# Gated mix of a long convolution and local attention: attention steps in another order, feature rows loaded instead of copied, and filters turned by VectorE

## The chip, the cores and the metric

One core of one Trainium2 chip. The metric is device time in microseconds, the median of several executions. A run is called slow when it is over 1.5% above the fastest of its kernel; slow runs stay out of all ratios, but medians and ranges are of all runs.

PE is TensorE, DVE VectorE, ACT ScalarE, POOL GpSimd, SP the engine whose queue issues most DMAs. The granted clock is the share of the full TensorE clock that was granted.

## The reference, cut to what matters

```python
def _A_ref(q, k, v, shift_k, ssm_k, ssm_D):          # S = 2048, D = 640
    k_shift = sum over t of k_pad[:, t:t+S, :] * shift_k[:, 3-t]     # 4-tap convolution
    kv = k_shift * v
    y = irfft(rfft(kv, 2*S) * rfft(ssm_k, 2*S))[:S].astype(bfloat16) # long convolution
    return q * (y + kv * ssm_D)

def _B_ref(x, wqkv, wo):                              # 32 heads of 20
    q, k, v = (x @ wqkv) split by head
    # each position attends to itself and the 7 positions 2, 4, ... 14 before it
    return softmax_attention(q, k, v) @ wo

g = sigmoid((x * gate_w).sum(-1, keepdims=True))      # x is A_q
out = g * A + (1 - g) * B
```

## The kernel before

The kernel computes v, then q and k (five column groups `ft` of 128), then attention in 24 steps, then the FFT as matmuls. Names that come again: PV is the product of the softmax weights and v, and `oS` its scaled result; `wo` are the weights of the output projection, `fin` its result before a DMA stores it to scratch memory; `kv` is the input of the convolution, `h` and `hn` are its filter rows, `G` and `T` constant matrices of the transform, `qg` rows of q that are scaled by the gate; stage 1 is the first product of the transform. Scores are matmuls over 31 rows: 20 of the head and 11 **feature rows**, whose product is zero inside the attention window and at most -256 outside it. So every head in the two q/k tiles `kq[0]` and `kq[1]` needs the same 11 rows beside its own 20. Before, four small DMAs put them in place for one head tile, and DVE copies them to the other seven:

```python
    def feats(e):
        kqt = pA.tile([128, 4, 2 * NSB, CB], BF, name=f"kq{e}", tag=f"K{e}")
        kq[e] = kqt
        if e == 0:
            nc.gpsimd.memset(kqt[:, 0], 0.0)
            for h4 in range(4):
                r = slice(32 * h4 + DH, 32 * h4 + DH + NF)          # DH = 20, NF = 11
                nc.sync.dma_start(kqt[r, 0].rearrange("p b c -> p (b c)"), ca["feat"].ap())

    def feat_copies(e):                                             # 14 copies in all
        for t in range(4):
            if e or t:
                for p in range(2):
                    ld.copy(kq[e][:, t, NSB * p:NSB * p + NSB], kq[0][:, 0, NSB * p:NSB * p + NSB], 800, eng="d")
                    ...
```

q and k go from PSUM into a staging tile `stg`, and from there by DMA to the rows of `kq`. The attention loop, with its fillers (late q/k, late v, output projection) after each step, and the loads for the FFT after step 7:

```python
    for k in range(len(steps)):               # (gi, t): gi = 0, 1, 2 and t = 0..7 in order
        if k + 1 < len(steps):
            scores(2 * k + 2); scores(2 * k + 3)
        pv(2 * k); pv(2 * k + 1)
        gi, t = steps[k]
        if gi == 0:
            advance(lqk, (3, 3, 2, 2, 0, 0, 0, 0)[t])
            advance(lv, (0, 0, 1, 2, 3, 3, 3, 0)[t])
        if k == NT - 1:
            ...                               # x and W leave memory, kv, G, h_lin take their place
            load_h(0)                         # 8 DMAs of 128-byte pieces, on the GpSimd queue
            nc.sync.dma_start(G[:], ...)
            for q in range(4):
                nc.sync.dma_start(kv[32 * q:32 * q + 32], ...)
            for g in range(1, NG):
                load_h(g)
        if opg is not None:
            advance(opg, 3 if t % 2 else 2)   # output projection of the gi before
        ...
```

The softmax here doesn't subtract the row's maximum and nothing guards it: scores larger than these inputs give would overflow.

Of the kernel before, what the change touches and what calls it, by code (L numbers as in the profile page):

```python
# [131 lines left out]
def kernel(  # L132
# [33 lines left out]
    Dz = p0.tile([128, 160], BF, name="Dz")  # L166
    g_nat = p0.tile([128, 16], F32, name="g_nat")
    omg = p0.tile([128, 16], F32, name="omg")

# [15 lines left out]
    pr = pB.tile([128, 4, 4 * D], BF, name="pr")  # L185
    v23 = pB.tile([128, 2, 4, D], BF, name="v23")
# [4 lines left out]
    def xs(m):  # L191
        return xS[:, m * D:(m + 1) * D]
# [5 lines left out]
    def load_x(m0, m1):  # L198
        for sub in range(2):
            for m in range(m0, m1):  # L200
                k0, k1 = (PRE if sub == 0 and m % 9 == 0 else 0), (KB - 2 if sub == 1 and m % 9 == 8 else KB)
                if (k0, k1) != (0, KB):
                    for i, n in split16(k1 - k0):
                        nc.sync.dma_start(xs(m)[KB * sub + k0 + i:KB * sub + k0 + i + n],
                                          raw(x2, xrow(2 * m + sub, k0 + i) * D, [[2 * D, n], [1, D]]))
            ms = [m for m in range(m0, m1) if not ((sub == 0 and m % 9 == 0) or (sub == 1 and m % 9 == 8))]
            a = ms[0]
            for b, nxt in zip(ms, ms[1:] + [-1]):
                if nxt != b + 1:
                    nc.sync.dma_start(xS[KB * sub:KB * sub + KB, a * D:(b + 1) * D].rearrange("p (m d) -> p m d", d=D),  # L210
                                      raw(x2, xrow(2 * a + sub, 0) * D, [[2 * D, KB], [4 * QB * D, b + 1 - a], [1, D]]))
                    a = nxt

    def load_w(w):
        nc.sync.dma_start(W[:, :, w, :], W3[:, :, w, :])

    kh = kvw[:, 0:19 * D].rearrange("p (t d) -> p t d", d=D)
    vns = [kvw[:, (19 + 4 * e) * D:(23 + 4 * e) * D].rearrange("p (t d) -> p t d", d=D) for e in range(2)] + [v23[:, 0], v23[:, 1]]

    def load_kv(c):  # L220
        if c == 0:
            nc.gpsimd.memset(kh[0:1, 0:3, :], 0.0)
            for p, n in ((1, 112), (113, 15)):
                nc.sync.dma_start(kh[p:p + n, 0:3, :], raw(k2, (16 * p - 3) * D, [[16 * D, n], [D, 3], [1, D]]))
        nc.sync.dma_start(kh[:, 3 + 4 * c:7 + 4 * c, :], raw(k2, 4 * c * D, [[16 * D, 128], [D, 4], [1, D]]))
        nc.sync.dma_start(vns[c], raw(v2, 4 * c * D, [[16 * D, 128], [D, 4], [1, D]]))

    nc.sync.dma_start(ident[:], ca["ident"].ap())
    for m in (0, 9):
        nc.gpsimd.memset(xs(m)[0:PRE], 0.0)  # L230
        nc.gpsimd.memset(xs(m + 8)[96:128], 0.0)
    load_x(0, 4); load_w(2); load_x(4, 9); load_x(9, 13)
# [3 lines left out]
    load_x(13, 18)  # L236
    load_kv(0)
    load_w(1); load_w(0)
    for c in range(1, 4):
        load_kv(c)  # L240
    nc.gpsimd.memset(Dz[:], 0.0)
    nc.gpsimd.tensor_copy(VW[:, :, :, DH], valid[:].unsqueeze(2).to_broadcast([128, 18, H]))
    for q in range(4):
        nc.gpsimd.dma_start(Dz[32 * q:32 * q + 1, :], A_ssm_D[160 * q:160 * q + 160].unsqueeze(0))
# [40 lines left out]
    def vproj_half(m, a, ps):  # L285
        for dt in range(NDT):
            nc.tensor.matmul(ps, lhsT=xT[:, dt, 128 * m:128 * m + 128], rhs=W[:, dt, 2, 320 * a:320 * a + 320],  # L287
                             start=(dt == 0), stop=(dt == NDT - 1))

    def vproj(m):  # L290
        ps = ppv.tile([128, 2, 512], F32, name="psv", tag="mm", bufs=3)
        for a in range(2):
            vproj_half(m, a, ps[:, a, 0:320])
# [31 lines left out]
    def feats(e):  # L325
        kqt = pA.tile([128, 4, 2 * NSB, CB], BF, name=f"kq{e}", tag=f"K{e}")
        kq[e] = kqt
        if e == 0:
            nc.gpsimd.memset(kqt[:, 0], 0.0)
            for h4 in range(4):  # L330
                r = slice(32 * h4 + DH, 32 * h4 + DH + NF)
                nc.sync.dma_start(kqt[r, 0].rearrange("p b c -> p (b c)"), ca["feat"].ap())

    def feat_copies(e):
        for t in range(4):
            if e or t:
                for p in range(2):
                    ld.copy(kq[e][:, t, NSB * p:NSB * p + NSB], kq[0][:, 0, NSB * p:NSB * p + NSB], 800, eng="d")
                    ld.t["d"] += 600
                    yield  # L340
# [16 lines left out]
    def qk_send(ft, stg):  # L357
        for h in range(H):
# [10 lines left out]
    def qk_gen():  # L369
        for ft in range(NDT - 1):  # L370
            stg = new_stg()
            for c in range(5):
# [3 lines left out]
                for part in range(2):  # L376
                    qk_evac(stg, c, part, ps[:, part])
                if c < 4:
                    yield
            if ft == 2:  # L380
                while advance(kvg, 1):
                    pass
                feats(1)
                for _ in feat_copies(1):
                    pass
            qk_send(ft, stg)
            yield

    def late_qk():
        stg = new_stg()  # L390
        for c in range(5):
            for part in range(2):
                ps = ppa.tile([128, 512], F32, name="pj2", tag="w", bufs=2)
                qk_part(NDT - 1, c, part, ps)
                qk_evac(stg, c, part, ps, eng="da"[part])
                if (c, part) == (4, 1):
                    qk_send(NDT - 1, stg)
                yield

    def late_v():  # L400
        for m in range(12, 18):
            for a in range(2):
                ps = ppa.tile([128, 512], F32, name="pv2", tag="w", bufs=2)
                vproj_half(m, a, ps[:, 0:320])
                ld.copy(VW[:, m, 16 * a:16 * a + 16, 0:DH], ps[:, 0:320].rearrange("p (h d) -> p h d", h=16), 320, eng="da"[a])
                yield
# [9 lines left out]
    def s1_gen(key, g):  # L416
        Am = p3.tile([128, 64, 4, IL], BF, name="Am", tag="Am", bufs=3)
        st[key] = Am
        for oc in range(4):
            ps = ps_tile("s1")  # L420
            psq = ps[:].rearrange("p a m -> p (a m)").rearrange("p (q l j) -> p q l j", q=4, l=4)
            for il in range(4):
                i = 4 * oc + il
                for qp in range(2):
                    rows = slice(64 * qp, 64 * qp + 64)
                    if key[0] == "h":
                        lhsT = h_lin[rows, IL * g + i].rearrange("p c n -> p (c n)")
                    else:
                        lhsT = kv[rows, :, :, IL * g + i].rearrange("p c n -> p (c n)")
                    nc.tensor.matmul(psq[:, 2 * qp:2 * qp + 2, il, :], lhsT=lhsT, rhs=F1b[rows, :], start=True, stop=True,  # L430
                                     tile_position=(64 * qp, 0), skip_group_check=True)
            ld.copy(Am[:, :, :, 4 * oc:4 * oc + 4], psq.rearrange("p q l j -> p j q l"), 1024)
# [56 lines left out]
    transposes(0)  # L489
    transposes(1)  # L490
    for m in range(12):
        vproj(m)
        transposes(m + 2)
        advance(kvg, 1)
    for m in range(14, 18):
        transposes(m)
    gate()
    feats(0)
    ld.t = dict(a=0.0, d=4000.0)
    qk = qk_gen(); fc = feat_copies(0)  # L500
    for k in range(20):
        advance(qk, 1)
        advance(kvg, 1)
        if k >= 3:
            advance(fc, 2)
        if k == 12:
            gate_end()
    while advance(kvg, 1):
        pass
# [6 lines left out]
    wo = pD.tile([128, NDT, D], BF, name="wo")  # L516
    nc.sync.dma_start(wo[:], B_wo.rearrange("(t p) n -> p t n", p=128))
# [8 lines left out]
    halves = [(gi, t, hf) for gi in range(NGI) for t in range(NT) for hf in range(2)]  # L526
# [48 lines left out]
    def op_tr(j):  # L575
# [4 lines left out]
        oT = pD.tile([128, NDT, 128], BF, name="oT", tag="oT", bufs=3)  # L580
# [47 lines left out]
    def load_h(g):  # L628
        for q in range(4):
            for c in range(2):  # L630
                nc.gpsimd.dma_start(h_lin[32 * q:32 * q + 32, IL * g:IL * g + IL, c, :],  # L631
                                  raw(A_ssm_k, (160 * q + 80 * c + IL * g) * S, [[64, 32], [S, IL], [1, 64]]))

    def tap0(g):
        r = h_lin[:, IL * g:IL * g + IL, :, 0]
        nc.vector.tensor_tensor(r, r, Dz[:].rearrange("p (c i) -> p i c", c=2)[:, IL * g:IL * g + IL], ALU.add)

    opg = None
    lqk, lv = late_qk(), late_v()
    steps = [(gi, t) for gi in range(NGI) for t in range(NT)]  # L640
    scores(0)
    scores(1)
    for k in range(len(steps)):
        if k + 1 < len(steps):
            scores(2 * k + 2)
            scores(2 * k + 3)
        pv(2 * k)
        pv(2 * k + 1)
        gi, t = steps[k]
        if gi == 0:  # L650
            advance(lqk, (3, 3, 2, 2, 0, 0, 0, 0)[t])
            advance(lv, (0, 0, 1, 2, 3, 3, 3, 0)[t])
        if k == NT - 1:
            sC.close()
            pF = ctx.enter_context(tc.tile_pool(name="pF", bufs=1, side="left", reuse_waits="tile"))
            kv = pF.tile([128, 2, 64, 80], BF, name="kv")
            G = pF.tile([128, 32, 2, 128], BF, name="G")
            h_lin = pF.tile([128, 80, 2, 64], BF, name="h_lin", tag="hl")
            load_h(0)
            nc.sync.dma_start(G[:], cf["G"].ap().rearrange("p (a r b) -> p a r b", a=32, r=2))  # L660
            for q in range(4):
                nc.sync.dma_start(kv[32 * q:32 * q + 32], raw(kvs, 2 * q * S * 80, [[64 * 80, 32], [S * 80, 2], [1, 5120]]))
            for g in range(1, NG):
                load_h(g)
        if opg is not None:
            advance(opg, 3 if t % 2 else 2)
        if t == NT - 1:
# [119 lines left out]
```

## Time and profile before

| | before |
|---|---|
| time, median of 4 runs beside the changed kernel | 336.3 us (333.7 to 337.8) |
| span of the profiled run, granted clock | 335.7 us, 0.813 |
| PE / DVE / ACT busy | 71% / 56% / 50% |
| DMA bytes | 46.23 MB |

The main readings are in the prediction below. The shares of the chain that ended last, from the page:

```profile
PE 35%; DVE 22%; DMA 13%; issue 12%; ACT 10%; SPq 5%; POOL 0%; DVEq 0%; ACTq 0%; POOLq 0%
```

"issue" is time in which an engine waited for nothing that the profile shows; a q after a name is that engine's sequencer. So 22% of the path is DVE and only 13% waits for transfers. The prediction calls stops of PE by issue late instructions, which is its guess: the page lists an instruction queue (43 packets, 0.70 MB), and no counter ties a stop to it. Second, the row of the feature rows in the list of DMA issues (the transfer, its queue and kind, how many, the size of one):

```profile
kq<-ca_feat SPq DMA_DIRECT2D x4, 93.6 KB
```

0.38 MB in all, which land from 48.2 to 51.2 us, at 128 GB/s (from the DMA view of that window).

### The profile page before, as it was taken

What the parts mean: (1) busy time and instruction counts of PE and PEld (TensorE: products, weight loads), DVE (VectorE), ACT (ScalarE), POOL (GpSimd) and SP (SyncE); (2) the same over time, 40 slices, a digit from 0 to 9 for tenths busy, and PEclk for the clock granted to TensorE, in tenths of its full rate; (3) what the DMA queues carried; (4) which work ended last, traced back from release to release, by engine and by line L of the source; (5) the groups of instructions that cost most, each with busy time, mean ns of one, the idle gap of its engine ahead of it and who ended that gap; (6) DMA issues with size and microseconds to landing.
All of it is one profiled execution on the core that took longest, in us unless ns stands there. A gap on an engine that the chain in (4) does not pass through costs nothing.

```text
span 335.7 us, 12259 instructions
## 1 busy us (share of the span) xinstructions
PE 238.3 (71%) x5549; PEld 175.0 (52%) x5556; DVE 188.4 (56%) x279; ACT 168.8 (50%) x247; POOL 52.9 (16%) x81
## 2 busy tenths in 40 slices
PE   1399899969549978643969987536696969677330
PEld 1277545535315655432746765536595958676320
DVE  0106999099924433211545555524949697973982
ACT  1167845355304544321546632625749595963670
POOL 7700231000200006235930000000000000000132
PEclk9999999999757997555877999567778797985855
DMA  6999953655375235997531112995503131397065
GB/s 174 227 220 361 415 140 94 144 120 145 108 146 129 56 85 199 212 199 159 130 96 31 43 53 85 206 234 139 129 2 87 45 86 44 66 221 159 19 164 138
DMA packets 16017, 46.23 MB, mean 138 GB/s; under 512 B 3811, under 2 KB 10833, under 8 KB 13872
## 3 DMA queue, kind: packets, MB, share of 16 engines
q1 hardware_dynamic: 13196, 38.14, 46.5%
q0 software_dynamic: 2768, 7.32, 8.3%
q8 instruction: 43, 0.70, 0.9%
q14 instruction: 10, 0.07, 0.1%
HBM read 26.75 MB, written 7.87 MB: 103 GB/s over the span
## 4 chain that ended last, share of the span: by engine, by line
PE 35%; DVE 22%; DMA 13%; issue 12%; ACT 10%; SPq 5%; POOL 0%; DVEq 0%; ACTq 0%; POOLq 0%
PE i L482 8%; PE op L595 6%; DVE pr L256 6%; PE s L445 5%; DMA kq<-stg 5%; ACT Am L119 4%; PE O L561 3%; DVE pr L260 3%; PE sc L539 3%; DMA xS<-in_A_q_dram 3%; PE pj L349 3%; DMA kvw<-in_A_k_dram 3%; DVE kq L121 3%; SPq L363 2%; ACT Up L119 2%
## 5 line engine op out<-in xcount | busy, mean ns | idle before, releaser
L349 PE MATMUL pj<-xT,W 128*128 128x456 bf16 (+3 forms) x243 | 50.9, 366 | 8.4 <-ACT stg L119 7.7
L542 ACT ACTIVATE ET<-sc 128x684 bf16<-128x684 f32 x48 | 33.3, 740 | 30.9 <-PE sc L539 28.7
L349 PEld LDWEIGHTS <-W 128*128 128x128 bf16 x250 | 24.8, 101 | 32.8 <-issue 13.2
L119 ACT CAST stg<-pj 128x456 bf16<-128x456 f32 (+3 forms) x45 | 21.4, 531 | 35.0 <-PE pj L349 17.7
L445 PE MATMUL s<-Am,G 64*128 64x64 bf16 x1280 | 25.6, 201 | 15.9 <-issue 11.6
L631 POOL DMA_DIRECT2D h_lin<-in_A_ssm_k_dram x40 | 25.8, 650 | 56.0 <-PE sc L539 40.3
L482 PE MATMUL i<-M,Hs 128*128 128x128 bf16 x160 | 28.9, 276 | 6.4 <-DVE Hs L469 4.3
L445 PEld LDWEIGHTS <-G 64*128 64x128 bf16 x1280 | 23.7, 103 | 17.4 <-issue 15.6
L256 DVE TENSOR_TENSOR pr<-kvw,wl 128x2560 bf16<-128x2560 bf16 x16 | 22.9, 1487 | 16.9 <-DMA kvw<-in_A_k_dram 16.8
L119 ACT CAST Am<-s 128x1024 bf16<-128x1024 f32 x25 | 24.1, 1060 | 12.8 <-PE s L430 8.4
L755 POOL DMA_DIRECT2D out_dram<-qg x12 | 6.0, 502 | 154.6 <-DVE qg L753 154.6
L482 PE MATMUL i<-M,Hw 128*128 128x128 bf16 x160 | 28.6, 276 | 0.4 <-DVE Hw L469 0.4
L595 PE MATMUL op<-wo,oT 128*128 128x320 bf16 x120 | 25.4, 359 | 3.8 <-ACT oT L582 2.3
L539 PE MATMUL sc<-kq 31*64 31x57 bf16 x1152 | 16.9, 206 | 14.6 <-issue 8.9
L482 PEld LDWEIGHTS <-Hs 128*128 128x128 bf16 x160 | 24.1, 159 | 5.1 <-DVE Hs L469 4.7
L568 DVE RECIPROCAL rd<-O 128x24 f32<-128x24 f32 x24 | 7.4, 306 | 34.5 <-PE O L561 34.5
L287 PEld LDWEIGHTS <-xT 128*128 128x128 bf16 x180 | 18.3, 105 | 14.1 <-issue 5.7
L539 PEld LDWEIGHTS <-kq 31*64 31x64 bf16 x1152 | 13.3, 115 | 22.9 <-issue 19.6
L482 PEld LDWEIGHTS <-Hw 128*128 128x128 bf16 x160 | 23.8, 158 | 2.6 <-DVE Am L121 1.1
L287 PE MATMUL psv<-W,xT 128*128 128x320 bf16 x120 | 20.8, 326 | 5.1 <-DMA W<-in_B_wqkv_dram 5.1
L119 ACT CAST Cm<-i 128x1024 bf16<-128x1024 f32 x13 | 13.1, 1012 | 19.7 <-PE i L482 19.7
L582 ACT COPY oT<-tr 128x640 bf16<-128x640 bf16 x18 | 12.5, 692 | 20.0 <-PE tr L579 19.7
(69 smaller groups left out, 409.9 us busy)
## 6 DMA issues: line engine op xcount, KB each, us to landing
Hw<-Hs SPq DMA_DIRECT2D x10, 512.0 KB
kq<-stg SPq DMA_DIRECT2D x28, 170.2 KB
kvw<-in_A_k_dram SPq DMA_DIRECT2D x4, 640.0 KB
kv_scr<-kvo POOLq DMA_DIRECT2D x4, 640.0 KB, 5.5
kv<-kv_scr SPq DMA_DIRECT2D x4, 640.0 KB
h_lin<-in_A_ssm_k_dram POOLq DMA_DIRECT2D x40, 64.0 KB, 4.0
qg<-in_A_q_dram SPq DMA_DIRECT2D x4, 640.0 KB
bl<-b_scr SPq DMA_DIRECT2D x4, 640.0 KB
```

Source lines behind the costliest of these rows:

```text
L119: self.nc.scalar.copy(dst, src)
L121: self.nc.vector.tensor_copy(dst, src)
L256: nc.vector.tensor_tensor(pr[:, j].rearrange("p (n c) -> p n c", n=4), kh[:, 4 * c + 3 - j:4 * c + 7 - j, :], wl[:, j, :].unsqueeze(1).to_ ...
L287: nc.tensor.matmul(ps, lhsT=xT[:, dt, 128 * m:128 * m + 128], rhs=W[:, dt, 2, 320 * a:320 * a + 320], start=(dt == 0), stop=(dt == NDT - 1))
L349: nc.tensor.matmul(ps[:, 0:nb * wd], lhsT=W[:, dt, which, 128 * ft:128 * ft + 128], rhs=rhs, start=(dt == 0), stop=(dt == NDT - 1))
L445: nc.tensor.matmul(o, lhsT=G[rows, j, r, :], rhs=Am[rows, 2 * j + r, :, :], start=(r == 0), stop=(r == 1), tile_position=(64 * c, 0), skip ...
L482: nc.tensor.matmul(o, lhsT=src[:, c, :, :, 8 * oc + il].rearrange("p q j -> p (q j)"), rhs=M[:, k, :], start=(k == 0), stop=(k == 1), skip ...
L539: nc.tensor.matmul(sc[64 * sub:64 * sub + 64, hh, QB * mb:QB * mb + QB], lhsT=kqt[r:r + DH + NF, t % 4, si, 0:KB], rhs=kqt[r:r + DH + NF, ...
L542: nc.scalar.activation(ETs[i % NET][:, :, 0:NW], sc[:, :, 0:NW], ACT.Exp, scale=SCALE)
L582: nc.scalar.copy(oT[:], tr[:])
L595: nc.tensor.matmul(op[:, 0:320], lhsT=oTs[j][:, ft, :], rhs=wo[:, ft, 320 * hf:320 * hf + 320], start=(ft == 0), stop=(ft == NDT - 1))
L631: nc.gpsimd.dma_start(h_lin[32 * q:32 * q + 32, IL * g:IL * g + IL, c, :], raw(A_ssm_k, (160 * q + 80 * c + IL * g) * S, [[64, 32], [S, IL ...
```

## The change

The intent is to take work off DVE before attention, to give PE work where it had stood still, and to prepare part of the FFT during attention. The core of the diff:

```diff
 def feats(e):
-        if e == 0:
-            nc.gpsimd.memset(kqt[:, 0], 0.0)
-            for h4 in range(4):
-                r = slice(32 * h4 + DH, 32 * h4 + DH + NF)
-                nc.sync.dma_start(kqt[r, 0]..., ca["feat"].ap())
-    def feat_copies(e): ...
+        for h4 in range(4):
+            nc.sync.dma_start(kqt[32 * h4 + DH:32 * h4 + DH + NF].rearrange("p t b c -> p t (b c)"),
+                              raw(ca["feat"].ap(), 0, [[2 * NSB * CB, NF], [0, 4], [1, 2 * NSB * CB]]))
 # q/k: three column groups before attention (was four), two inside (was one); all v before
-        for ft in range(NDT - 1):
+        for ft in range(NDT - 2):
...
+        feats(1)
+        qk_send(NDT - 3, stg, 1)
 # steps by halves of the heads, so the second q/k tile is first needed in step 8
-    halves = [(gi, t, hf) for gi in range(NGI) for t in range(NT) for hf in range(2)]
+    steps = ([(0, t) for t in range(4)] + [(1, t) for t in range(4)] + [(0, t) for t in range(4, 8)]
+             + [(1, t) for t in range(4, 8)] + [(2, t) for t in range(8)])
 # filters: full rows, then 20 DVE transposes; stage 1 of two groups early, in attention
-    def load_h(g): ...        # 128-byte pieces
+    def load_hn(g):
+        nc.sync.dma_start(hn[:], raw(A_ssm_k, IL * g * S, [[80 * S, 8], [S, IL], [1, S]]))
+    def ht_gen():
+        for g in range(NG):
+            nc.vector.tensor_tensor(hns[g][:, 0:1], hns[g][:, 0:1], D5[:, g:g + 1], ALU.add)
+            for p in range(4):
+                nc.vector.transpose(hT[:, g]..., hns[g][:]...)
+                ...
 # one quarter of kv at the start of each of steps 10-13, of G of 14-17; qg and T later, in the FFT body
+        if 10 <= k < 14:
+            nc.sync.dma_start(kv[32 * q:32 * q + 32], ...)
+        if 14 <= k < 18:
+            nc.sync.dma_start(G[32 * q:32 * q + 32], ...)
 # fillers woven between the halves of scores and PV
+        if nxt: scores(2 * k + 2)
+        fill(0)
+        if nxt: scores(2 * k + 3)
+        fill(1)
+        pv(2 * k)
+        fill(2)
+        pv(2 * k + 1)
+        fill(3)
+        if k >= 1: advance(ht, 1)
```

Cut: x and W loaded in another order, memory placement, late values (all v is now computed first).

## The prediction

> **What bounds the kernel now.** I first read the page's busy shares: TensorE (PE) is busy 71% of the span, VectorE (DVE) 56%, ScalarE (ACT) 50%. Nobody is full on average, so the bound changes by stage. I cut the span where the groups of instructions change and asked for busy time, granted clock and DMA share by stretch. The columns are the stretch, its length, each engine's busy us with its count of instructions, clock, DMA share, GB/s.
> ```profile
> 0.00:40.00 40.00, 26.30 (x217) 19.20 (x218) 13.05 (x9) 20.44 (x31) 12.68 (x20) 1.00 0.97 273
> 40.00:98.50 58.50, 47.03 (x374) 24.85 (x378) 45.69 (x42) 25.02 (x51) 8.49 (x9) 0.91 0.54 136
> 98.50:128.40 29.90, 27.16 (x682) 16.49 (x687) 11.65 (x29) 12.43 (x21) 0.00 (x0) 0.84 0.40 88
> 128.40:157.00 28.60, 15.32 (x519) 10.80 (x520) 6.84 (x19) 9.38 (x14) 12.94 (x20) 0.56 0.97 219
> 157.00:196.00 39.00, 34.09 (x1247) 24.70 (x1246) 20.44 (x54) 20.94 (x31) 12.83 (x21) 0.84 0.28 73
> 196.00:208.90 12.90, 10.44 (x92) 7.54 (x91) 6.44 (x12) 4.15 (x6) 0.00 (x0) 1.00 0.26 74
> 208.90:237.00 28.10, 15.73 (x496) 14.57 (x497) 14.00 (x18) 14.36 (x15) 0.00 (x0) 0.65 0.75 176
> 237.00:311.00 74.00, 55.98 (x1424) 51.98 (x1424) 53.68 (x76) 50.72 (x55) 0.00 (x0) 0.81 0.43 95
> 311.00:335.70 24.70, 6.26 (x512) 4.89 (x511) 16.54 (x27) 11.31 (x25) 5.96 (x12) 0.60 0.41 109
> ```
> I call these rows load, q/k, attention in three parts, output tail, FFT start, FFT body and end. Two rows stand out: 128-157 and 209-237, where no engine is busy much over half, the DMA share is 0.97 and 0.75, and the clock is 0.56 and 0.65. The rows of output tail, FFT body and end are hardly touched by the change.
>
> For the q/k stage I read the chain in order of time. From 29.7 to 91.8 it runs through DVE (pr L256, L260, L263, kvo L265 and the feature copies kq L121), broken by a wait of DVE on the sends to kq. The PE timeline shows what PE does meanwhile:
> ```profile
> 71.18 12.55 PE L349 MATMUL pj<-xT,W 128*128 128x512 bf16 x69 [2.67 <-ACT stg L119]
> 83.65 0.69 PE L539 MATMUL sc<-kq 31*64 31x57 bf16 x48
> ...
> 89.69 3.81 PE L349 MATMUL pj<-xT,W 128*128 128x512 bf16 x9 [0.34 <-issue]
> 98.50 2.29 PE L349 MATMUL pj<-xT,W 128*128 128x512 bf16 x5 [5.00 <-ACT stg L119]
> ```
> PE has its first scores at 83.65, does one step, and then waits to 98.50: the staging tile is not sent, because the send stands behind the eight feature copies into the second kq tile (DVE, 86.9 to 92.5), which stand behind the k/v convolution.
>
> For the middle I read the PE timeline again:
> ```profile
> 140.53 0.60 PE L539 MATMUL sc<-kq 31*64 31x57 bf16 x39
> 146.56 0.33 PE L539 MATMUL sc<-kq 31*64 31x57 bf16 x9 [5.43 <-issue]
> ...
> 150.22 0.39 PE L561 MATMUL O<-VW,ET 64*64 64x21 bf16 x13
> 155.50 0.66 PE L561 MATMUL O<-VW,ET 64*64 64x21 bf16 x35 [4.90 <-issue]
> ```
> PE stops in the middle of a run of equal matmuls, waiting for nothing that the profile shows. Between the two stops it ran about 133 matmuls with their weight loads, some 266 instructions. The FFT start has the same: 6.73 us at 216.6, while 3.6 MB of qg and T are loading, and 2.03 at 232.
>
> [...] 0.50 granted in 139-159. [...] The 40 h_lin loads are 128 B runs; the page counts 3811 packets under 512 B, and POOL waits 14.9 us on its own earlier ones. [...]
>
> **The change, part by part.** TensorE's instruction count is the same (11,114 rows in both programs); only the order changes.
>
> *Load and q/k stage, ending at the first steady attention step.* Removed from DVE: 14 feature copies of 753 ns = 9.7 us; features come by four DMAs per kq tile. The staging copies of this stage go to ACT alone (about 1.15 us a chunk against 1.95 us of PE, so off the path). DVE is left with the convolution, 22.9 + 11.3 + 6.0 + 6.0 + 1.5 = 48 us, starting a little earlier because k is loaded before the last x blocks: done by about 75. PE becomes the bound: first value matmul near 13 (W, as before); 18 blocks at 1.64 us (the timeline's spacing) + 2.5 us at half clock - 2 for transposes made ahead = 30, so 43; gate 4.7; then three of the five q/k column groups (before four) = 150 matmuls x 195 ns (127 in 24.69 us) = 29.3. Scores start near 77 to 80, and no stop at 89-98 follows, since the second kq tile isn't needed before step 8. Before, 98.5 had about 2.5 us of attention already done, so it stood for 96. Gain about **16 us**, with 6 value blocks more and one q/k group less in it (60 x 173 ns = 10.4 against 50 x 210 = 10.5: nothing).
>
> *Attention, 97.5 us before.* Work of PE at full clock: a step's scores and PV take 1.0 us (0.50 + 0.50 by the timeline), 24 of them 24; projections of gi 0 and 1, 24 halves of 0.8 and 12 transposes of 0.4, 24; late q/k 100 x 0.21 = 21; early FFT stage 1 of h, 8 units of 0.45 = 3.6. Sum 73. By steps: 0-7, 3.7 each = 29.5. Steps 8-11 hold no filler and are bound by sends: before, the last two score groups of head tiles 6 and 7 waited until 5.9 and 10.9 us after the last late q/k copy, hidden by value filler; now nothing hides them, so about 13 for 4 us of work. Steps 12-15, 4.1 each = 16.5. Then wo, h rows and kv (3.2 MB) come in one go behind those sends, some 16 us at 200 GB/s; at the old rate of stop per burst (12 of 28.6 us) that is 6 us of late instructions, and 2 us of half clock. Steps 16-23, 3.2 to 3.4 each = 27: op 1.5 + scores/PV 1.0 + stage 1 0.45, and waits on two shared PSUM buffers. The DVE transposes, 20 of 128x512, [...] one a step, where DVE has 1.0 (reciprocal and scaling) to 2.5 us of other work a step of 3 to 4. Mostly beside PE. Sum 94; gain **3 to 10 us**, say 5.
>
> *FFT start, 28.1 + 1.8 us of wait on the tap sums before it.* Stage 1 of h groups 0 and 1 and their copies leave (3.6 + 3.4), the 1.8 goes, and the 6.7 stop goes. What remains, two interleaved runs, took 4 and 8.7 us: 13. Gain 17. The qg/T burst moves to the start of the FFT body, where the first 10 us need few instructions: I give back 5 there. Net **12**.
>
> Output tail, end: 0. Moving the G load to quarters among the stores costs some us on the store queue, none on PE. POOL's 25.8 us of h_lin issue is off the path. Sum 16 + 5 + 12 = 33 of 337: **304 us**.
>
> **Rivals.** (1) *Only the stop moves*: bursts of the same 46 MB starve PE elsewhere (steps 10-15 and FFT body), and steps 8-11 idle on the sends. For: the same bytes, filler gone there. Against: G is cut in four, 128 B runs are gone, bursts are shorter than 28 us. It would leave 16 + 0 + 5: 316. (2) *DVE or PSUM turns-around bind attention*: transposes at 1.2 us or more, stage 1 copies in strided 512-element halves, one O buffer that waits for DVE. Steps 16-23 at 4.5 us, and 1-15 a little longer: attention 104, time 314. (3) *Everything hides*: the instruction stops vanish and the clock stays full; attention 80, FFT start 12 with 2 given back: 286.
>
> **Range and chances.** 304 stands between rivals 1 and 2 (314 to 316) and rival 3 (286), which I think less likely as step 8's hole is in the program order. 8 in 10: 291 to 317. For less than 2% gain both q/k and FFT start must fail: 4%.
>
> **What would show it.** Right: scores start at 77 to 82 and go on without a 9 us hole; DVE's convolution ended before; the hole sits in steps 8-11 behind kq sends; stops by issue sum to less than half of the page's 12% of the chain; FFT start near 13 us; transposes near 1 us. Wrong: stage one ends past 88 (loads or the wait for the features bind); transposes over 1.5 us on the chain; issue stops of 5 us or more still there twice in attention; clock under 0.8 in steps 12-23.

## The result and the profile after

The changed kernel took **381.1 us** (379.7 to 387.5, 4 runs) against 336.3 before on the same chip: a ratio of 1.133, 95% interval 1.123 to 1.143. It is slower. A ratio here is the mean time of one kernel's fast runs over that of the other's of the same rounds, so it is not quite the ratio of the medians.

The two profiles, cut into the same stages (us; before: span 335.7, after: 377.5). "Scores start" before is counted as 96 instead of 83.65, because of the stop that followed. The FFT start ends here at the first matmul of the inverse, so it is longer than the prediction's row of that name.

| stage | before | after | change | predicted change |
|---|---|---|---|---|
| to the start of steady scores | 96.0 | 95.3 | -0.7 | -16 |
| attention | 100.0 | 150.3 | **+50.3** | -5 |
| output tail | 12.9 | 12.4 | -0.5 | 0 |
| FFT start | 34.8 | 19.5 | -15.3 | -17 |
| FFT body | 68.2 | 77.2 | +9.0 | +5 |
| end | 23.8 | 22.8 | -1.0 | 0 |

So the FFT side came about as predicted, and the loss is all before it. The page's shares of the last chain after:

```profile
PE 37%; DMA 29%; DVE 10%; ACT 9%; issue 8%; SPq 4%; POOL 0%; POOLq 0%; DVEq 0%; ACTq 0%
```

DVE fell from 22% to 10%, as the change intends, and waiting for transfers rose from 13% to 29%. The list of DMA issues (the transfer, its queue and kind, how many, the size of one) says what is new:

```profile
kq<-ca_feat SPq DMA_DIRECT2D x8, 374.3 KB
```

The features are now 3.1 MB instead of 0.38: eight loads, each of 11 partitions times four head tiles. The chain in order of time (start us, us, what) has them, and what stood behind them in the same queue:

```profile
58.54 16.98 DMA kq<-ca_feat
75.54 12.81 DMA kq<-stg
...
99.08 9.86 DMA kq<-ca_feat
108.96 21.73 DMA hn<-in_A_ssm_k_dram
```

From 58 to 88 the path is the first set of feature loads and the staging sends after it. From 99 to 131 it is the second set, then the first load of filter rows. PE's timeline (start, us, line, operation, in brackets the idle time before and what ended it) shows the price:

```profile
89.53 5.82 PE L336 MATMUL pj<-xT,W 128*128 128x512 bf16 x20 [10.67 <-ACT stg L120]
95.27 0.68 PE L554 MATMUL sc<-kq 31*64 31x57 bf16 x48
...
133.64 0.82 PE L576 MATMUL O<-VW,ET 64*64 64x21 bf16 x48 [18.96 <-DVE oS L586]
...
176.85 0.53 PE L554 MATMUL sc<-kq 31*64 31x57 bf16 x23 [9.13 <-issue]
```

Three stops, 38.8 us together (10.67 + 18.96 + 9.13). The second one looks like a wait for DVE, but DVE's timeline shows that DVE was itself waiting:

```profile
130.81 0.16 DVE L496 TENSOR_TENSOR hn<-hn,D 128x1 bf16<-128x1 bf16 x1 [22.30 <-DMA hn<-in_A_ssm_k_dram]
131.01 1.03 DVE L498 STREAM_TRANSPOSE hT<-hn 128x512 bf16<-128x512 bf16 x1
131.97 0.65 DVE L122 CAST stg<-pj 128x512 bf16<-128x512 f32 x1
132.54 0.29 DVE L583 RECIPROCAL rd<-O 128x24 f32<-128x24 f32 x1
132.87 0.72 DVE L586 TENSOR_TENSOR oS<-O,rd 128x240 bf16<-128x240 f32 x2
```

The first filter transpose is placed after step 1. DVE works in program order, so when the filter rows are late, the small scaling `oS` that PE needs waits 22 us behind a transpose that nobody needs for 100 us. **A prefetch became a wait on the critical path because its consumer shares an in-order engine with urgent work.**

How fast the feature loads are is read from windows of the changed kernel's profile (stretch, length, busy of PE, PEld, DVE, ACT, POOL, clock, DMA share, GB/s):

```profile
66.00:70.00 4.00, 4.00 (x21) 1.88 (x20) 3.97 (x2) 1.99 (x5) 0.00 (x0) 1.00 0.76 87
70.00:74.00 4.00, 3.95 (x26) 2.34 (x25) 3.59 (x6) 2.31 (x6) 0.56 (x1) 1.00 0.65 74
...
118.00:122.00 4.00, 0.00 (x0) 0.00 (x0) 0.00 (x0) 0.00 (x0) 0.00 (x0) 0.58 0.62 80
...
167.00:209.00 42.00, 27.40 (x592) 17.07 (x586) 16.14 (x34) 11.12 (x17) 0.00 (x0) 0.60 0.64 126
209.00:245.60 36.60, 32.08 (x807) 21.57 (x807) 23.57 (x51) 17.51 (x29) 0.00 (x0) 0.72 0.24 59
```

In the first three rows transfers run at 74 to 87 GB/s with a DMA share of 0.62 to 0.76. The last two rows are about steps 12 to 15 and 16 to 23: the clock is 0.60 and 0.72, with PE busy for 88% of the time in the last one.

From 102 to 122 the queue of these loads alone moved 80 GB/s, at a share of 0.68 of the 16 DMA engines. In the windows with little other traffic the trace has 74 to 96 GB/s, and the 1.53 MB of the first set (4 x 374.3 KB) take 17 us of the chain. My estimate from these is 19 us a set: 1.53 MB at 80 GB/s. But the kernel before wrote its four small loads into the same rows of the four blocks at 128 GB/s, so these rows alone do not explain the rate. What sets it is not shown: no run here isolates it.

### The profile page after: what moved, and what is told of

It reads as the page before. It is cut to its first block, busy times and chain, and to the rows that moved or that the text cites. A ratio compares the mean times of both kernels' runs of the same rounds, so it can differ in the third digit from the quotient of the medians.

```text
span 377.5 us, 12172 instructions
## 1 busy us (share of the span) xinstructions
PE 253.0 (67%) x5545; PEld 178.9 (47%) x5556; DVE 200.7 (53%) x292; ACT 167.1 (44%) x245; POOL 21.0 (6%) x38
## 2 busy tenths in 40 slices
DMA packets 14057, 48.91 MB, mean 130 GB/s; under 512 B 3327, under 2 KB 6783, under 8 KB 11605
## 4 chain that ended last, share of the span: by engine, by line
PE 37%; DMA 29%; DVE 10%; ACT 9%; issue 8%; SPq 4%; POOL 0%; POOLq 0%; DVEq 0%; ACTq 0%
PE i L480 8%; DMA xS<-in_A_q_dram 7%; DMA kq<-ca_feat 7%; PE op L610 7%; DMA hn<-in_A_ssm_k_dram 6%; DMA kq<-stg 5%; PE pj L336 5%; PE psv L289 4%; DMA b_scr<-fin 4%; ACT Am L120 3%; PE O L576 3%; PE s L443 3%; PE sc L554 2%; SPq L350 2%; ACT Up L120 2%
## 5 line engine op out<-in xcount | busy, mean ns | idle before, releaser
L336 PE MATMUL pj<-xT,W 128*128 128x456 bf16 (+3 forms) x239 | 54.8, 375 | 12.0 <-ACT stg L120 11.0
L120 ACT CAST stg<-pj 128x456 bf16<-128x456 f32 (+3 forms) x40 | 19.2, 528 | 61.9 <-PE pj L336 45.3
L610 PE MATMUL op<-wo,oT 128*128 128x320 bf16 x120 | 29.6, 401 | 7.6 <-DVE fin L615 3.4
L256 DVE TENSOR_TENSOR pr<-kvw,wl 128x2560 bf16<-128x2560 bf16 x16 | 22.8, 1486 | 19.1 <-DMA kvw<-in_A_k_dram 19.0
L554 PE MATMUL sc<-kq 31*64 31x57 bf16 x1152 | 19.4, 211 | 20.1 <-issue 11.3
L576 PE MATMUL O<-VW,ET 64*64 64x21 bf16 x1152 | 19.8, 192 | 19.5 <-DVE oS L586 19.5
L576 PEld LDWEIGHTS <-ET 64*64 64x64 bf16 x1152 | 15.9, 129 | 32.5 <-issue 30.5
L289 PE MATMUL psv<-W,xT 128*128 128x320 bf16 x180 | 29.8, 320 | 0.9 <-DMA W<-in_B_wqkv_dram 0.9
L615 DVE CAST fin<-op 128x320 bf16<-128x320 f32 x24 | 11.8, 490 | 33.7 <-PE op L610 27.5
L120 ACT CAST Hs<-s 128x1024 bf16<-128x1024 f32 x19 | 18.8, 1025 | 15.4 <-PE s L443 15.3
L122 DVE CAST stg<-pj 128x512 bf16<-128x512 f32 (+1 forms) x10 | 6.3, 632 | 32.5 <-PE pj L336 30.6
## 6 DMA issues: line engine op xcount, KB each, us to landing
kq<-ca_feat SPq DMA_DIRECT2D x8, 374.3 KB
```

Source lines behind the costliest of these rows:

```text
L120: self.nc.scalar.copy(dst, src)
L256: nc.vector.tensor_tensor(pr[:, j].rearrange("p (n c) -> p n c", n=4), kh[:, 4 * c + 3 - j:4 * c + 7 - j, :], wl[:, j, :].unsqueeze(1).to_ ...
L289: nc.tensor.matmul(ps[:, a, 0:320], lhsT=xT[:, dt, 128 * m:128 * m + 128], rhs=W[:, dt, 2, 320 * a:320 * a + 320], start=(dt == 0), stop=( ...
L336: nc.tensor.matmul(ps[:, 0:nb * wd], lhsT=W[:, dt, which, 128 * ft:128 * ft + 128], rhs=rhs, start=(dt == 0), stop=(dt == NDT - 1))
L554: nc.tensor.matmul(sc[64 * sub:64 * sub + 64, hh, QB * mb:QB * mb + QB], lhsT=kqt[r:r + DH + NF, t % 4, si, 0:KB], rhs=kqt[r:r + DH + NF, ...
L576: nc.tensor.matmul(O[64 * par:64 * par + 64, s, 21 * sl:21 * sl + 21], lhsT=ET[rows, hh, QB * mb:QB * mb + 64], rhs=VW[rows, NMB * gi + mb ...
```

## The experiments

Twelve kernels in four calls, each timed beside the kernel before on the same chip (334.3 to 335.2 us). All gave the reference's result. Theory A was that the feature loads, by the time they hold the queue, are the main cause; the main rival was that what stands behind them (filter rows placed too early on DVE) or the collision of later loads is.

| run | what it is | us, median | ratio to before [95%] |
|---|---|---|---|
| changed kernel | | 381.1 | 1.133 [1.123, 1.143] |
| e1_hn_first | filter rows queued ahead of the second feature set | 385.3 | 1.135 [1.123, 1.147] |
| e2_feat_copies | features as before: 4 loads, 14 copies | 351.1 | 1.048 [1.039, 1.057] |
| e3_feat_distinct | same feature loads from eight distinct sources | 382.7 | 1.138 [1.126, 1.151] |
| b2_feat_loads | kernel before, feature loads alone | 351.0 | 1.050 [1.044, 1.055] |
| e4_late_kv | e2, kv and G queued later | 338.9 | 1.013 [1.008, 1.017] |
| e5_unwoven | e2, fillers in one block | 352.7 | 1.054 [1.046, 1.063] |
| b1_fft_half | kernel before, FFT side alone | 357.8 | 1.070 [1.063, 1.077] |
| e6_s1_in_hole | e4, early stage 1 moved to steps 8-11 | 338.0 | 1.007 [0.999, 1.016] |
| e7_pool_stores | e6, output stores on the GpSimd queue | 352.9 | 1.060 [1.052, 1.067] |
| e8_qg_spread | e7, qg and T loads cut up | 346.4 | 1.033 [1.026, 1.041] |
| e9_am_first | e6, stage 1 results in other memory | 341.0 | 1.018 [1.011, 1.026] |
| e10_am_spread | e9, qg and T loads cut up | 332.2 | 0.979 [0.971, 0.988] |

### e2_feat_copies: the features as before, in the changed kernel

```diff
-        for h4 in range(4):                      # 4 loads of 374 KB per q/k tile
-            nc.sync.dma_start(kqt[32 * h4 + DH:32 * h4 + DH + NF]..., ...)
+        if e == 0: ...                           # 4 loads of 94 KB for one head tile
+    def feat_copies(e): ...                      # 14 DVE copies, as in the kernel before
```

> Changed kernel with the features made as before: four small loads (94 KB each) and 14 DVE copies of 753 ns (10.5 us on DVE, which has room after 74). Theory A: both stops (10.7 and 19) go or shrink to a few us: 381 minus 27 to 31, so 350 to 355, still slower than before (336), the rest being attention. Theory B: at most 10 us gained, 371 or more.

Measured 351.1 us, 30 less than the changed kernel, where the theory put it. In its profile (fast, span 344.9) scores start at 83.81 instead of 95.27, the two stops of 10.67 and 18.96 are 1.63 and 3.13, and attention takes 127 us instead of 150. So putting 9.7 us of DVE copies back gains 30 us. But it still loses 16 to the kernel before. By stages it now has 83.8 us to the scores (before: 96.0), 21.0 in the FFT start (34.8), 77.5 in the FFT body (68.2), and 127 in attention (100): without the feature loads, 12 of the 16 us that the prediction gave to the first stage are there, and what is lost is lost in attention. Its timeline shows where to look next:

```profile
145.17 0.53 PE L568 MATMUL sc<-kq 31*64 31x57 bf16 x22 [7.69 <-issue]
```

That stop stands in a window in which the DMA share is full and no engine does much:

```profile
137.20:145.20 8.00, 0.31 (x14) 0.15 (x6) 2.12 (x5) 0.05 (x1) 0.00 (x0) 0.50 1.00 174
```

### e1_hn_first: does the late filter load alone cost the 19 us?

```diff
+        load_hn(0)
+        load_hn(1)
         feats(1)
         qk_send(NDT - 3, stg, 1)
```

> Changed kernel with one edit: the first two loads of conv-kernel rows (hn) are queued ahead of the second feature load instead of behind it. Theory A (the queue: DVE waits in order for hn behind 1.5 MB of slow feature rows, and PE waits for DVE's scaling): the 19 us stop of PE before the second PV goes, the 10.7 us stop of the q/k stage stays; 381 falls by 14 to 19, to 362 to 367. Theory B (the woven order, late instructions and the cold clock are what costs, the wait for hn only happens to be where it shows): the gap reappears elsewhere, 375 to 381.

Measured 385.3 us: no gain, and theory A missed. The gap came back elsewhere, as theory B said, though in the main behind the same queue and not by the order of the work. The wait for `hn` fell from 22.30 to 2.79 us, but the second feature set still held the queue, and now the next staging send stood behind it. In place of the one stop of 18.96 PE has one of 7.01 by issue (at 115.8, unexplained) and one of 13.72 for that send. The timelines of PE and of DVE:

```profile
139.49 2.29 PE L336 MATMUL pj<-xT,W 128*128 128x512 bf16 x5 [13.72 <-ACT stg L120]
...
139.02 0.69 DVE L122 CAST stg<-pj 128x512 bf16<-128x512 f32 x1 [23.04 <-DMA kq<-stg]
```

This is the more useful lesson of the two: the 19 us were not the fault of what waited. Whatever stands behind 20 us of slow queue waits: `hn` for 22.30 us in the changed kernel, the staging send for 23.04 here.

### e3_feat_distinct: is it the source?

The changed loads read the same 96 KB four times each, with a repeat in the access pattern. A rival was that reading the same addresses makes them slow.

```diff
-  raw(ca["feat"].ap(), 0, [[2 * NSB * CB, NF], [0, 4], [1, 2 * NSB * CB]])
+  raw(ca["featx"].ap(), (4 * e + h4) * NF * 8 * NSB * CB, [[8 * NSB * CB, NF], [2 * NSB * CB, 4], [1, 2 * NSB * CB]])
```

> Changed kernel whose eight feature loads read eight different contiguous copies from memory (34,848 B a row) instead of reading one 8.7 KB row four times over, 32 loads of the same 96 KB in all. Same bytes, same 11 destination partitions[...]. If the source (repeated reads of one small region) is what makes them slow: a set lands in under 9 us instead of 17, the stops shrink, 352 to 362. If it is the writing of long rows into single partitions[...]: a set still takes 15 us or more, 378 to 383.

Measured 382.7, as the changed kernel, and the first set still takes 16.26 us in its chain (the profile fell on a slow run). Not the source: what remains is the bytes and the rows that they are written to, which no run here tells apart.

### b2_feat_loads: the feature loads alone, on the kernel before

The edit of e2 in reverse, on the kernel before.

> The kernel before with only the feature part of the change: eight loads of 374 KB instead of four of 94 KB and 14 DVE copies. If the queue time of these loads (17 and 20 us) is what costs by itself: 350 to 362. If it only costs with the new order: 333 to 340 (10 us of DVE copies are gone).

Measured 351.0: the feature loads alone cost 16 us there. The chain in order of time, where the kernel before had DVE work:

```profile
72.88 10.20 DMA kq<-stg
83.10 22.90 DMA kq<-ca_feat
106.01 8.39 DMA kq<-stg
```

In the changed kernel the same loads cost 30. More stands behind them there (filter rows, two late column groups), which I take for the reason; no run tests it.

### e4_late_kv: the loads that collide in steps 8 to 11

In e2 the kv quarters are queued from step 10 on, while the last staging sends and filter rows still run.

```diff
-        if 10 <= k < 14: ... kv quarter          # ahead of the step's work
-        if 14 <= k < 18: ... G quarter
+        if 12 <= k < 16: ... kv quarter          # after the step's work and stores
+        if 17 <= k < 21: ... G quarter
```

> The run with feature copies (351) with one edit more: the four kv loads are queued after the stores of steps 12 to 15 instead of right behind wo and the conv rows before step 12, the four G loads after those of steps 17 to 20. Theory (a burst in one go [...]holds the output stores behind it): the 7.7 us stop by issue at step 11 falls under 3, the 5.6 us wait for a store goes, the clock of steps 12-15 rises from 0.67: 336 to 343. Rival (the holes belong to the step order; the loads are incidental): 348 to 352.

Measured 338.9, 12 less than e2 in ratio terms (1.048 to 1.013), as expected. Of the three signs, two came in the profile (a slow run, span 347.4): 0.27 us in place of the 7.69 us stop by issue, and a clock of 0.80 from 150 to 176. The third didn't: the wait on `fin` stayed (6.52, before 5.62).

### e5_unwoven: does the weaving of fillers matter?

```diff
-        cut = [len(units) * j // 4 for j in range(5)]
+        cut = [0, 0, 0, 0, len(units)]
```

> The run with feature copies (351) with the weaving undone: all fillers of a step in one block after its second PV, as before the change, same order of steps. If the weaving costs (small runs between transposes and projections, the clock cold at 0.67 to 0.79 in steps 12 to 23): 346 or less, clock above 0.85 there. If it is neutral: 349 to 353. If it helps, 354 or more.

Measured 352.7 against 351.1 for e2 (ratios 1.054 and 1.048, intervals overlapping): nothing that shows.

### b1_fft_half: the FFT side alone, on the kernel before

Filter rows and DVE transposes, early stage 1, kv and G in quarters, late qg and T, all on the kernel before. To fit into memory it also loads `wo` later and keeps two `oT` buffers instead of three.

> The kernel before with only the FFT side of the change: conv rows turned by DVE transposes, early stage 1 of two groups, kv and G loads spread, qg and T loaded after the first products; features, q/k stage and attention order as before. If that half is good as predicted: FFT start 28 to 35 us falls by 13 to 15, attention loses some of its 12 us of stops, the FFT body gives back 6 to 9 (late qg/T burst): 335 falls to 317 to 326. If transposes and early stage 1 cost attention as much as they save: 331 to 338.

Measured 357.8, 32 above the range for a good half and 20 above the one for a bad half, and partly my own doing: `wo` now stood in the queue behind the filter rows. PE's timeline:

```profile
144.43 1.49 PE L633 MATMUL op<-wo,oT 128*128 128x320 bf16 x5 [9.42 <-DMA wo<-in_B_wo_dram]
```

The FFT start did shrink to 20 us, as in the changed kernel. But steps 16 to 23, which carry the early stage 1, took 46 us against 25 before (from the PV of step 15 to that of step 23), with the output projection at 1.49 us a group where the kernel before, at a granted clock of 1.00 (window 185.8 to 188.5), takes 0.85. The early stage 1 is not free filler: part of the FFT start's gain is paid back in attention. How much of the 21 us more is clock and how much is the shared PSUM buffers, this run doesn't tell apart.

### e6_s1_in_hole and e9_am_first: filling the hole of steps 8 to 11

Steps 8 to 11 wait for the last sends. e6 moves the eight units of early stage 1 there; e9 also moves their results to memory that no send is still reading.

```diff
+    for k in range(4):
+        plan[8 + k] = [("s", 2)]                 # e6; taken from steps 16-23
```

> The run with late kv (339) with the eight early stage 1 units moved from steps 16-23 to steps 8-11, two a step, where PE waits for the kq sends. If those steps are a hole (14 us for 4 us of work) and the units cost 1 us or more each in steps 16-23 (shared PSUM buffers): 329 to 334. If they only fill a hole that the next wait reopens, or delay the sends: 336 to 341.

```diff
             wo = pF.tile([128, NDT, D], BF, name="wo")
+            for j in range(2):                   # e9: ahead of kv and G, so over x, not over stg
+                amb = pF.tile([128, 64, 4, IL], BF, name=f"Amp{j}", tag=f"Am{j}")
+                ams.append(amb)
```

> This is e6_s1_in_hole with its first two Am tiles placed lower in memory, over the transposed x, which is free once the late q/k matmuls are done, and no longer over the staging tiles, which the sends are still reading. Theory A (the hole in steps 8 to 11 stayed in e6 because stage 1 had to wait for the sends to finish reading the memory it writes to): the waits of 11.0 us (PE for Am) and 10.6 us (DVE on kq from stg) go, the eight stage 1 units, about 8 us of PE with their waits, fill the hole, and the time falls by 4 to 9 us from 338 to 329-334. Rival B (the next step in the hole waits for the same sends, for the last heads' rows of the second kq tile, so nothing is gained however the hole is filled, and stage 1 has only changed places): less than 3 us, 335-340.

e6: 338.0, the same as e4. Its waits (what, us in total, times, longest) show that stage 1 could not start, because its result lay over the staging tiles, which the sends were still reading:

```profile
PE s1e L435 <- ACT Am L120: 11.0, 1, 11.0
DVE Am L122 <- DMA kq<-stg: 10.6, 1, 10.6
```

e9: 341.0, no gain either, though those waits are gone. Both are cut here at 127.2, near the first early unit, at the first output projection, and at 199.0, where both have just done the PV of step 22 (198.7 and 198.4); e6 is the first fence (slow run), e9 the second:

```profile
127.20:153.50 26.30, 13.63 (x527) 11.07 (x516) 14.94 (x30) 11.93 (x21) 0.00 (x0) 0.61 0.46 96
153.50:199.00 45.50, 39.19 (x1168) 26.19 (x1169) 27.68 (x62) 20.88 (x31) 0.00 (x0) 0.81 0.61 151
```

```profile
127.20:148.30 21.10, 12.65 (x462) 9.98 (x453) 14.16 (x27) 11.37 (x19) 0.00 (x0) 0.62 0.56 120
148.30:199.00 50.70, 40.73 (x1164) 26.64 (x1165) 28.29 (x63) 20.89 (x31) 0.00 (x0) 0.76 0.56 134
```

The hole is 5.2 us shorter, and the steps after it 5.2 us longer. Of these PE is busy for 1.5 (40.73 for 39.19) and idle for 3.7: two stops by issue of 1.83 and 1.69 stand there where e6 has one of 1.22. The clock is lower too, 0.76 for 0.81. Why is open.

### e7_pool_stores and e8_qg_spread

The waits for `fin` end when stores to scratch, on the same queue as kv and G, are done. Both runs build on e6. e7 moves the stores to the GpSimd queue; e8 also cuts the burst of qg and T in the FFT body into single loads.

```diff
-                nc.sync.dma_start(raw(b_scr[:], ...), fins[j]...)      # e7
+                nc.gpsimd.dma_start(raw(b_scr[:], ...), fins[j]...)
```

> The run before it with the output stores queued by GpSimd instead of on the queue of the loads. If the waits of DVE's fin copy for a store (9.1 and 5 us, PE idle 6.5) come from the stores standing behind kv and conv-row loads in one queue: 5 to 8 us less than the run before it (322 to 328). If the DMA engines themselves are full: no more than 2 us less.

```diff
-            for g4 in range(4): qg quarter g4;  then T                 # e8
+            load_qg(0)      # quarters 1, 2, 3 and T later, one at a time through the FFT body
```

> The run before it with the late burst of the FFT body (2.6 MB qg and 1 MB T in one go) cut into four qg loads and one T load, one each half group. If that burst starves PE (6.1 to 6.7 and 1.7 us by issue, and a cold clock after): 6 to 10 us less, 313 to 321, below the kernel before (334). If not: within 2 us.

e7: 352.9, 15 **worse**. Without stores between them, nothing holds the kv and G loads back: SP issues all eight from 150.2 to 159.8 us, where in e6 they are spread from 159.8 to 192.5. A window of that burst, and the wait on `fin` that was to go:

```profile
145.00:176.00 31.00, 18.13 (x414) 11.72 (x415) 11.96 (x25) 9.85 (x15) 6.26 (x12) 0.66 0.83 169
...
169.91 1.49 PE L624 MATMUL op<-wo,oT 128*128 128x320 bf16 x5 [10.49 <-DVE fin L629]
```

The shared queue had been the pacing. That the burst is what costs the 15 us, and not the issue of the stores by GpSimd, is my reading; no run separates the two. e8: 346.4, 6.5 less than e7 by the medians and 8.7 by the means of the fast runs, as expected (6 to 10): the late burst in the FFT body costs about that.

### e10_am_spread: all parts together

e9 with the cut-up qg and T loads of e8.

> e9_am_first plus the qg and T loads cut up through the FFT body, as in e8. Theory A: the burst at the start of the FFT body costs its 6 us here as well, so 5 to 8 us below e9_am_first of the same call. If A holds for both, 322-329, which would be below the kernel before (334 to 336) by 2 to 4%. Rival B: the loads collide later instead with stage 1 and the b_scr stores, less than 3 us.

Measured 332.2 us, 8.9 below e9 by the medians and 11.9 by the means of the fast runs, more than the 5 to 8 expected. The absolute 322 to 329 was missed by the median; the three fast runs have 328.4, 328.8 and 332.2. It is 49 us faster than the changed kernel. Against the kernel before the ratio of fast runs is 0.979, interval 0.971 to 0.988, which leaves out two of its five runs, 335.3 and 335.8, as slow, though their clocks (0.853 and 0.823) are no lower than those of the others; with all runs the means are 332.1 and 335.5. **So it is 1 to 2% below the kernel before, which the record calls unclear.** It is the changed kernel with the features copied by DVE, kv and G later, stage 1 in steps 8 to 11, and qg and T spread.

## Why the prediction was wrong

It said 304, and left 4% for less than 2% of gain; it was 381. In the two profiles the time rose by 41.8 us where it said a fall of 33: an error of 75, of which 15 stand before the scores, 55 in attention and 6 in the FFT, less 1.5 in the output tail and the end.

**The step that failed** is the one sentence "features come by four DMAs per kq tile". It counted the 9.7 us of DVE copies that go, and gave the loads no duration. They move 3.1 MB at 74 to 96 GB/s, some 17 us a set, and hold the queue that the staging sends and the filter rows pass through. Giving the copies back returns 30 us (e2); adding the loads to the kernel before costs 16 (b2). The bytes were in the diff. An estimate from the trace of the kernel before, 1.53 MB at the 128 GB/s of its small feature loads, would have been 12 us a set; some 17 were measured. This step is 30 of the 75 us; the other large part is the two mis-sized terms of attention below.

**"Scores start near 77 to 80, and no stop"**: 95.3, with a stop of 10.67 before it. With the features copied, scores start at 83.8, so the rest of the step was 4 to 7 us off: PE's first matmul came at 10.7 us (kernel before: 7.3), and the gate ended at 54.0 where the prediction had 47.7. DVE's convolution was done at 73, as predicted (75).

**Attention, "sum 94"**: 150.3. Steps 0 to 7 took 56.3 for 29.5: 19.0 of it is the stop on the filter rows, which the prediction had as DVE work "mostly beside PE". The size of the transposes was right (1046 ns each, the mean of 20, where the list of signs has "near 1 us"); that they stand in DVE's order ahead of PE's next release was not thought of. Steps 8 to 11, "about 13": 15.4, the mechanism held. Steps 12 to 15 took 42.0 for 24.5, with one stop by issue of 9.1 where 6 was allowed, a wait on `fin`, and a clock of 0.60 where 2 us of half clock were allowed. Steps 16 to 23 took 36.6 for 27, at a clock of 0.72. These two terms were mis-sized by 27 us together (the cut at 209.0 between them is good to about 1.5 us). Moving kv and G away from the sends gives 12 of the total back (e4).

**FFT start, "gain 17"**: 15.3, right, though a stop by issue of 3.89 stayed there; b1 shows the gain on the other kernel as well. **"I give back 5"** in the FFT body: 9.0 measured, and cutting the burst up returns 8.7 (e8 against e7) and 11.9 (e10 against e9) by the means of the fast runs.

**Rival 1**, that only the stop moves, was nearest to what happened in kind, but it too had no term for the features. All three rivals only made the gain smaller or larger, and none asked what an added transfer might do. The list of signs did: "stage one ends past 88 (loads or the wait for the features bind)" came true, but had no cost and no chance beside it. A clock under 0.8 in steps 12 to 23 came true as well; slow transposes didn't, and of the stops by issue of 5 us or more in attention there was one, not two.

**Two readings in it are off.** It sets the 3811 packets under 512 B beside the `h_lin` loads; the changed kernel has none of these loads and still 3327 such packets, so most were not theirs. And between the two stops of 5.43 and 4.90 the lines have 128 matmuls, not about 133; with their weight loads that is 256 instructions, not some 266.

What stays open: why the clock stays low in steps 12 to 23 (in steps 16 to 23 it was 0.72 with PE busy for 32.1 of 36.6 us, while the kernel before had 0.84 in its last part of attention with PE busy for 34.1 of 39.0), and how the loss of 16 us that e2 still has is split beyond the 12 of the kv and G loads. The new order of the steps was never run alone on the kernel before, so its share in the 127 us of attention isn't known. That stops by issue are late instructions remains an inference; no counter shows what PE waits for. In runs of equal matmuls there are stops of 5.4 and 4.9 us in the kernel before, 9.1 in the changed kernel and 7.7 in e2, at a DMA share of 0.98 to 1.01, but also of 3.9 and 6.1 us in the changed kernel, at 0.42 and 0.63, and of 7.0 in e1, at 0.72. The one of e2 went when the DMA load around it was moved (7.69 to 0.27 in e4), but one of 3.7 to 4.0 us stands at the FFT start of the changed kernel and of all ten e runs, at a DMA share of only 0.41 to 0.45.

## What to carry to other kernels

Give every added DMA a duration before counting what it replaces: its bytes over a rate that the trace shows for such rows (74 to 96 GB/s for the loads of 374.3 KB here), and ask what stands behind it in its queue. Here 14 copies of 0.75 us on VectorE were cheaper than eight loads into 11 rows (351.1 us in e2 against 381.1). Place the consumer of a prefetch, on an engine that works in order (VectorE here: the wait for `hn` held `oS` for 22 us), only where the data will surely be there. When several loads compete with small urgent sends, where each is queued was worth more here than what fills the engines: the time went from 381 to 351, 339 and 332 us by removing or moving transfers, and moving the stores off the queue that had paced the loads cost 15.
